# A hash-attention and mixture-of-experts kernel: expert tiles behind a condition, weights by change of expert

## The chip, the cores and the metric

One core of one Trainium2 chip runs the whole program in one launch. The metric is the device time of one execution in microseconds (us); lower is better. The time of the kernel before is the median of three runs. A measurement of this kernel tells about 0.2% from no change.

## The reference

Two blocks follow each other. The first is attention with 4 batches, 8 heads, 768 positions and head width 64, in which a query sees only keys of the same hash bucket. The second sends each of the 3072 tokens (width 512) to the one of 8 experts whose embedding it is most similar to.

```python
q_bits = einsum(q, proj) > 0;  k_bits = einsum(k, proj) > 0      # 6 bits: a bucket
mask = q_bucket[..., :, None] == k_bucket[..., None, :]
attn = softmax(where(mask, q @ k.T / sqrt(D), -1e9))
x = (attn @ v).transpose(0, 2, 1, 3).reshape(3072, 512)
logits = normalized(x) @ normalized(expert_emb).T / tau          # 8 experts
expert_idx = argmax(logits);  gate_w = softmax(logits)[expert_idx]
for e in range(8):
    out[expert_idx == e] = gate_w * (relu(x @ w1[e]) @ w2[e])    # 512 -> 1024 -> 512
```

With the inputs that the reference sets up (a fixed seed), it sends 464, 461, 375, 317, 367, 377, 373 and 338 tokens to the experts 0 to 7.

## The kernel before

**Attention** (lines 166 to 358) takes 16 pairs of heads, each in 12 units of work. A table `todo` in the source says after which unit a pair's loads (`load`), features, hash bits and output (`finish_half`) are issued. SyncE's queue issues the loads of q, k and v; ScalarE makes a pass over a pair's q and k (line 239) and the exps (line 274); TensorE makes the scores (lines 268, 271) and the products with v (line 289). `route` picks an expert for each token and writes the batch's rows, with the gate weight as column 513, to a table `xd` in device memory (line 160).

**The branch.** A general attention, `attention_any`, is needed only when q and k are large. One flag, `beyond_i`, is read into a register by every engine, and a condition (line 446) jumps past that code. With these inputs it isn't run.

**The routing table** (lines 450 to 519) sorts the tokens by expert. TensorE counts (`cnt`, `rank`), VectorE works out for each expert its number of 128-token tiles (`tiles`), their running end (`tend`) and each tile's expert (`texp`), and 24 matmuls (line 516) put the token numbers into slots; `src` (line 519) holds, for each of NT = 31 tiles, 128 row numbers of `xd`. 31 is what 3072 tokens can need at most when each expert's last tile is partly filled. An empty slot points to a row of zeros, and its result is not written.

**The expert tiles** (lines 522 to 576) run 31 times. `fetch(t)` reads the tile's expert into a register of SyncE, loads that expert's `w1t` and `w2t` (2 MB each, lines 535 and 537, two buffers each), and gathers 128 token rows by an indirect DMA of GpSimd (line 539, three buffers). `turn_x` transposes them on TensorE (line 549) and copies them out (VectorE, line 551). 32 products with `w1t` (line 563) go through a Relu on ScalarE in two halves (line 566); 8 products with `w2t` follow (line 571); VectorE scales by the gate weight (`y`, line 573), and GpSimd scatters the rows to the output (line 574). A tile issues `fetch(t + 2)` and `turn_x(t + 1)` between its two products. An fp32 product is two matmul instructions in the trace: 64 of line 563 and 16 of line 571 for a tile.

The pools of weights lie where attention's buffers lay, so no weight load is issued before the routing table is done.

Of the kernel before, what the change touches and what calls it, by code (L numbers as in the profile page):

```python
# [25 lines left out]
def kernel(  # L26
# [26 lines left out]
    NT = (N + E * (P - 1)) // P  # L53
    XW = DM + 1
# [30 lines left out]
    iota_t = iota("iota_t", [P, NT], [[1, NT]])  # L85
# [30 lines left out]
    for h in range(2):  # L116
        for r in range(2):
            c0 = h * D + r * NB
            nc.sync.dma_start(proj2[h * D : (h + 1) * D, c0 : c0 + NB], proj[:, :])

    oh_all = const.tile([P, E, NBLK], F32, name="oh_all")

# [43 lines left out]
    with ExitStack() as at:  # L166
# [3 lines left out]
        op = pool("op", 2, at)  # L170
# [5 lines left out]
        def banks():  # L176
            return ps_w.tile([P, 2, 512], F32, name="banks", tag="banks")
# [4 lines left out]
        for i in range(NPT):  # L182
            t = ep.tile([P, 2, SH + 2], F32, name=f"p{i}")
# [164 lines left out]
        for u in range(U + LAG + 3):  # L348
            if u < U:
                scores(u)  # L350
            if 0 <= u - LAG < U:
                attend(u - LAG)
            for f, *args in todo.get(u, ()):
                f(*args)


        most = rp.tile([P, 1], F32, name="most", tag="most")
        nc.vector.reduce_max(out=most[:], in_=squares[:], axis=AX.X)
        ps = banks()
# [4 lines left out]
                                op0=ALU.is_gt)  # L364
        beyond_i = const.tile([1, 1], I32, name="beyond_i")
# [77 lines left out]
                nc.vector.tensor_copy(out=l[:], in_=lg[:])  # L443
                route(b, x, l, rp)

    with tc.If(nc.values_load(beyond_i[0:1, 0:1], min_val=0, max_val=1) > 0):
        attention_any()


    with ExitStack() as so:  # L450
        sp = pool("sp", 1, so)
# [13 lines left out]
                                in1=iota_n[:].unsqueeze(1).broadcast_to([P, E, NBLK]), op=ALU.is_gt)  # L465
        tiles = sp.tile([P, E], F32, name="tiles")
        nc.vector.reduce_sum(out=tiles[:], in_=full[:], axis=AX.X)
        tend = sp.tile([P, E], F32, name="tend")
        nc.vector.tensor_tensor_scan(out=tend[:], data0=ones[:, 0:E], data1=tiles[:], initial=0.0,
                                     op0=ALU.mult, op1=ALU.add)  # L470
# [3 lines left out]
                                in1=tend[:, 0 : E - 1].unsqueeze(1).broadcast_to([P, NT, E - 1]), op=ALU.is_ge)  # L474
        texp = sp.tile([P, NT], F32, name="texp")
        nc.vector.reduce_sum(out=texp[:], in_=past[:], axis=AX.X)
        texp_i = const.tile([P, NT], I32, name="texp_i")
        nc.vector.tensor_copy(out=texp_i[:], in_=texp[:])


        tstart = sp.tile([P, E], F32, name="tstart")
# [6 lines left out]
                                op=ALU.add)  # L488
# [17 lines left out]
                                in1=rf[:].unsqueeze(2).broadcast_to([P, NBLK, P]), op=ALU.is_equal)  # L506
        col = sp.tile([P, NBLK, NT], F32, name="col")
        nc.vector.tensor_tensor(out=col[:], in0=iota_t[:].unsqueeze(1).broadcast_to([P, NBLK, NT]),
                                in1=tf[:].unsqueeze(2).broadcast_to([P, NBLK, NT]), op=ALU.is_equal)
        nc.vector.tensor_tensor(  # L510
            out=col[:], in0=col[:],
            in1=tok[:].rearrange("p b c -> p (b c)").unsqueeze(2).broadcast_to([P, NBLK, NT]), op=ALU.mult,
# [5 lines left out]
        src = const.tile([P, NT], U32, name="src")  # L518
        nc.vector.tensor_scalar_add(src[:], slot[:], float(N))


    wp = pool("wp", 2)
    gp = pool("gp", 3)
    hp = pool("hp", 2)
    ps_x = pool("ps_x", 2, space=PSUM)
    ps_h = pool("ps_h", 2, space=PSUM)
    ps_y = pool("ps_y", 2, space=PSUM)
    got = {}

    def fetch(t):  # L530
        if t >= NT:
            return
        e = nc.values_load(texp_i[0:1, t : t + 1], engines=(mybir.EngineType.SP,), min_val=0, max_val=E - 1)
        a = wp.tile([P, ND, F], F32, name="w1t", tag="w1t")
        nc.sync.dma_start(a[:], w1[bass.ds(e, 1), :, :].rearrange("o (c p) f -> p (o c) f", p=P))
        b = wp.tile([P, NF, DM], F32, name="w2t", tag="w2t")
        nc.sync.dma_start(b[:], w2[bass.ds(e, 1), :, :].rearrange("o (c p) m -> p (o c) m", p=P))
        x = gp.tile([P, XW], F32, name="xg", tag="xg")
        nc.gpsimd.indirect_dma_start(out=x[:], out_offset=None, in_=xd[:, :],  # L539
                                     in_offset=bass.IndirectOffsetOnAxis(ap=src[:, t : t + 1], axis=0))  # L540
        got[t] = a, b, x

    def turn_x(t):
        if t >= NT:
            return
        a, b, x = got[t]
        ps = ps_x.tile([P, DM], F32, name="ps_x", tag="ps_x")
        for d in range(ND):
            nc.tensor.transpose(ps[:, d * P : (d + 1) * P], x[:, d * P : (d + 1) * P], ident[:])  # L549
        xt = hp.tile([P, ND, P], F32, name="xgt", tag="xgt")  # L550
        nc.vector.tensor_copy(out=xt[:], in_=ps[:].rearrange("p (d n) -> p d n", n=P))  # L551
        got[t] = a, b, x, xt

    fetch(0)
    fetch(1)
    turn_x(0)
    for t in range(NT):
        a, b, x, xt = got.pop(t)
        ht = hp.tile([P, NF, P], F32, name="ht", tag="ht")
        ps = ps_h.tile([P, NF, P], F32, name="ps_h", tag="ps_h")  # L560
        for f in range(NF):
            for d in range(ND):
                nc.tensor.matmul(ps[:, f, :], lhsT=a[:, d, f * P : (f + 1) * P], rhs=xt[:, d, :],  # L563
                                 start=(d == 0), stop=(d == ND - 1))
            if f % 4 == 3:
                nc.scalar.activation(ht[:, f - 3 : f + 1, :], ps[:, f - 3 : f + 1, :], ACT.Relu)  # L566
        fetch(t + 2)
        turn_x(t + 1)
        py = ps_y.tile([P, DM], F32, name="ps_y", tag="ps_y")
        for f in range(NF):  # L570
            nc.tensor.matmul(py[:], lhsT=ht[:, f, :], rhs=b[:, f, :], start=(f == 0), stop=(f == NF - 1))  # L571
        y = gp.tile([P, DM], F32, name="y", tag="y")
        nc.vector.tensor_scalar_mul(y[:], py[:], x[:, DM : DM + 1])  # L573
        nc.gpsimd.indirect_dma_start(out=out[:, :],  # L574
                                     out_offset=bass.IndirectOffsetOnAxis(ap=src[:, t : t + 1], axis=0),
                                     in_=y[:], in_offset=None, bounds_check=N - 1, oob_is_err=False)


# [28 lines left out]
```

## Time and profile before

| | before |
|---|---|
| median of 3 runs | 1033.05 us (1031.98 to 1033.67) |
| the profiled execution, its own time | 1033.62 us |
| its span, first to last instruction | 1031.9 us |
| attention, up to the flag `beyond_i` | 512 us of the span |
| branch and routing table, up to `src` | 512 to 545 us |
| expert tiles, to the last scaling `y` | 545 to 1024 us |
| TensorE busy | 966.8 us (94%) |
| weights loaded for the tiles | 31 times 4 MB |

Times in the profile count from the first instruction. PE is TensorE's matmuls, PEld its weight loads, DVE VectorE, ACT ScalarE, POOL GpSimd, SP SyncE; a q behind a name is that engine's sequencer or DMA queue. PEclk is the granted clock, 1.00 for 2.4 GHz and 0.50 for 1.2 GHz.

### The profile page before, as it was taken

How to read it: one execution, taken by the hardware profiler on the slowest of the kernel's cores; microseconds unless marked ns; L12 is line 12 of the kernel's file. 1: busy time of each engine (PE TensorE's matmuls, PEld its weight loads, DVE VectorE, ACT ScalarE, POOL GpSimd, SP SyncE). 2: the span in 40 equal slices, each digit the busy share in tenths (PEclk: the TensorE clock that was granted, in tenths of full speed). 3: DMA queues.
4: the chain of work that ended last, by engine and by line, in shares of the span. 5: the costliest groups of instructions: out<-in, count | busy, mean ns of one | idle time of the engine just before them, and what ended most of it. 6: DMA issues, size and time to landing. Idle time of an engine off the chain costs nothing. (4 is left out here: it accounts for less than half of the span.)

```text
span 1031.9 us, 13121 instructions
## 1 busy us (share of the span) xinstructions
PE 966.8 (94%) x5477; PEld 574.0 (56%) x5477; DVE 321.0 (31%) x550; ACT 244.9 (24%) x357; POOL 70.0 (7%) x81
## 2 busy tenths in 40 slices
PE   4999999999999999999736999999999999999996
PEld 2444444444444444444335667766766776677674
DVE  3545546554555456455430000100110010011000
ACT  3443444343544335333300000000000000000000
POOL 1000000000000000000001101110110111011000
PEclk8999999999999999999956999999999999999999
DMA  8111013111121112000018988888898888888860
GB/s 184 31 47 46 17 46 107 32 47 47 31 93 47 31 47 77 1 1 1 1 63 313 353 320 310 311 313 316 314 311 317 312 314 312 320 307 314 304 253 1
DMA packets 109121, 170.57 MB, mean 165 GB/s; under 512 B 53302, under 2 KB 57398, under 8 KB 108545
## 3 DMA queue, kind: packets, MB, share of 16 engines
q1 hardware_dynamic: 104064, 155.23, 45.3%
q0 software_dynamic: 4992, 14.44, 3.5%
q8 instruction: 45, 0.74, 0.3%
q14 instruction: 20, 0.16, 0.0%
HBM read 157.06 MB, written 14.43 MB: 166 GB/s over the span
## 5 line engine op out<-in xcount | busy, mean ns | idle before, releaser
L563 PEld LDWEIGHTS ps_h<-xgt,w1t 128*128 128x128 f32 x1984 | 230.5, 193 | 32.4 <-ACT ht L566 18.1
L563 PE MATMUL ps_h<-xgt,w1t 128*128 128x128 f32 x1984 | 236.5, 278 | 10.8 <-ACT ht L566 10.8
L571 PE MATMUL ps_y<-w2t,ht 128*128 128x512 f32 x496 | 218.0, 592 | 0.0
L274 ACT ACTIVATE p<-banks 128x768 f32<-128x768 f32 x192 | 154.0, 808 | 219.6 <-PE banks L271 194.9
L268 PE MATMUL banks<-qt,kt 64*128 64x384 f32 x768 | 177.4, 539 | 0.2 <-ACT p L274 0.2
L289 PE MATMUL av<-p,vt 128*64 128x385 f32 x768 | 166.4, 512 | 0.1
L281 DVE TENSOR_TENSOR acc<-acc,p 128x768 f32<-128x768 f32 x128 | 122.6, 958 | 116.0 <-ACT p L274 114.9
L571 PEld LDWEIGHTS ps_y<-w2t,ht 128*128 128x128 f32 x496 | 91.9, 190 | 103.8 <-issue 103.8
L566 ACT ACTIVATE ht<-ps_h 128x512 f32<-128x512 f32 x62 | 37.0, 597 | 464.2 <-PE ps_h L563 464.2
L573 DVE TENSOR_SCALAR y<-ps_y,xg 128x512 f32<-128x512 f32 x31 | 23.3, 751 | 323.8 <-PE ps_y L571 323.8
L268 PEld LDWEIGHTS banks<-qt,kt 64*128 64x128 f32 x768 | 58.7, 187 | 81.9 <-issue 77.7
L289 PEld LDWEIGHTS av<-p,vt 128*64 128x64 f32 x768 | 38.0, 134 | 91.9 <-issue 89.2
L271 PE MATMUL banks<-qb,kb 64*128 64x384 bf16 x384 | 63.6, 325 | 0.0
L574 POOL DMA_INDIRECT out_dram<-y,src x31 | 31.5, 1015 | 409.4 <-DVE y L573 409.4
L551 DVE COPY xgt<-ps_x 128x512 f32<-128x512 f32 x31 | 21.5, 692 | 110.8 <-PE ps_x L549 100.3
L312 PEld LDWEIGHTS banks<-ones,acc 128*128 128x128 f32 x384 | 51.5, 191 | 0.0
L310 PE MATMUL banks<-iden,o 128*128 128x144 f32 x192 | 47.9, 331 | 0.7 <-DVE o L295 0.7
L312 PE MATMUL banks<-ones,acc 128*128 128x1 f32 x384 | 48.2, 229 | 0.0
L295 DVE TENSOR_SCALAR o<-av 128x384 f32<-128x384 f32 x32 | 19.8, 618 | 68.4 <-PE av L289 68.4
L310 PEld LDWEIGHTS banks<-iden,o 128*128 128x128 f32 x192 | 28.9, 190 | 20.0 <-issue 18.6
L150 POOL TENSOR_TENSOR nrm<-ss,half 128x6 f32<-128x6 f32 x4 | 5.3, 1334 | 488.3 <-ACT sq L132 488.3
L243 PE MATMUL banks<-ident,qk 128*128 128x128 f32 x192 | 29.1, 291 | 8.1 <-DMA qk<-in_q_dram 8.1
(119 smaller groups left out, 417.2 us busy)
## 6 DMA issues: line engine op xcount, KB each, us to landing
w1t<-in_moe_w_dram SPq DMA_DIRECT2D x31, 2048.0 KB, 9.4
w2t<-in_moe_w_dram SPq DMA_DIRECT2D x31, 2048.0 KB, 11.1
xd<-xb SPq DMA_DIRECT2D x4, 1539.0 KB, 5.9
qk<-in_q_dram SPq DMA_DIRECT2D x32, 192.0 KB, 3.6
qk<-in_k_dram SPq DMA_DIRECT2D x32, 192.0 KB, 3.9
vt<-in_v_dram SPq DMA_DIRECT2D x16, 384.0 KB, 3.6
xg<-xd,src POOLq DMA_INDIRECT x31, 7.6
out_dram<-y,src POOLq DMA_INDIRECT x31, 7.7
```

The source lines that it names most:

```text
L243: nc.tensor.transpose(ps[:, c // HC, (c % HC) * P : (c % HC + 1) * P], qk[:, i, c, :, :], ident[:])
L268: nc.tensor.matmul(ps[:, h, 0:SH], lhsT=kt[rows[h], c // HC, kc], rhs=qt[rows[h], s, :], start=True, stop=False)
L271: nc.tensor.matmul(ps[:, h, 0:SH], lhsT=kb[rows[h], c // HC, kc], rhs=qb[rows[h], s, :], start=False, stop=True)
L274: nc.scalar.activation(p[:, :, 0:SH], ps[:, :, 0:SH], ACT.Exp, scale=ESCALE)
L281: nc.vector.tensor_tensor(out=a[:], in0=a[:], in1=p[:, :, 0:SH], op=ALU.add)
L289: nc.tensor.matmul(ps[h * D : (h + 1) * D, 0 : SH + 1], lhsT=vt[:, h, c, :], rhs=p[:, h, 0 : SH + 1], start=(c == 0), stop=(c == NC - 1))
L310: nc.tensor.matmul(t[:, c, :], lhsT=o[:, cols], rhs=iden[:, j, :], start=True, stop=True)
L312: nc.tensor.matmul(z[:, c, h : h + 1], lhsT=a[:, h, cols], rhs=ones[:, 0:1], start=True, stop=True)
L563: nc.tensor.matmul(ps[:, f, :], lhsT=a[:, d, f * P : (f + 1) * P], rhs=xt[:, d, :], start=(d == 0), stop=(d == ND - 1))
L566: nc.scalar.activation(ht[:, f - 3 : f + 1, :], ps[:, f - 3 : f + 1, :], ACT.Relu)
L571: nc.tensor.matmul(py[:], lhsT=ht[:, f, :], rhs=b[:, f, :], start=(f == 0), stop=(f == NF - 1))
L574: nc.gpsimd.indirect_dma_start(out=out[:, :], out_offset=bass.IndirectOffsetOnAxis(ap=src[:, t : t + 1], axis=0), in_=y[:], in_offset=None ...
```

## The change

The weights get four fixed buffers, `w1s` and `w2s`, two each, that live from the start. Expert 0's weights are loaded into all four without a condition, by statements inside the attention loop (after units 48 and 72; a load has no other work to wait for, so the scheduler sets its place in the queue). Six small VectorE steps make three more tables: `live` (tiles that hold tokens), `need` (live tiles whose expert is another than that of the tile two before, whose buffer they take over; for the first two, another than expert 0) and `nt` (the number of live tiles). A weight load is issued for every tile but carried out only if `need` says so (`cond`). It is issued when the buffer's last reader in the tile before is past. Tiles 0 to 23 run as they did; each of tiles 24 to 30 stands inside a condition `nt > t`, nested in that of the tile ahead. The general attention's condition gets `preferred_fallthrough_block=False`: the code of the case that is not run then stands behind the short other case, where before it stood ahead of it. The other pools become fixed turns of as many buffers as before.

```diff
+    NW = 2
+    w1s = [const.tile([P, ND, F], F32, name=f"w1_{i}") for i in range(NW)]
+    w2s = [const.tile([P, NF, DM], F32, name=f"w2_{i}") for i in range(NW)]
+    def bring1(i, e=0, **kw):
+        nc.sync.dma_start(w1s[i][:], w1[bass.ds(e, 1)].rearrange("o (c p) f -> p (o c) f", p=P), **kw)
...
+            if u in (4 * PU, 6 * PU):
+                bring1(u // (2 * PU) - 2)
+                bring2(u // (2 * PU) - 2)
...
-    with tc.If(nc.values_load(beyond_i[0:1, 0:1], min_val=0, max_val=1) > 0):
+    with tc.If(nc.values_load(beyond_i[0:1, 0:1], min_val=0, max_val=1) > 0, preferred_fallthrough_block=False):
         attention_any()
...
+        live = sp.tile([P, NT], F32, name="live")
+        nc.vector.tensor_scalar(out=live[:], in0=iota_t[:], scalar1=tend[:, E - 1 : E], scalar2=None, op0=ALU.is_lt)
+        need = sp.tile([P, NT], F32, name="need")
+        nc.vector.tensor_scalar(out=need[:, 0:NW], in0=texp[:, 0:NW], scalar1=0.0, scalar2=None, op0=ALU.not_equal)
+        nc.vector.tensor_tensor(out=need[:, NW:NT], in0=texp[:, NW:NT], in1=texp[:, 0 : NT - NW], op=ALU.not_equal)
+        nc.vector.tensor_tensor(out=need[:], in0=need[:], in1=live[:], op=ALU.mult)
...
+        nc.vector.tensor_copy(out=nt_i[:], in_=tend[:, E - 1 : E])
...
+    def expert_of(t):
+        e, n = (nc.values_load(a[0:1, t : t + 1], engines=(mybir.EngineType.SP,), min_val=0, max_val=m)
+                for a, m in ((texp_i, E - 1), (need_i, 1)))
+        return e, n > 0
...
+    def expert_tile(t):
...
+        more = t + NW < NT
+        if more:
+            e, needed = expert_of(t + NW)
+            bring1(t % NW, e, cond=needed)
         fetch(t + 2)
         turn_x(t + 1)
...
+        if more:
+            bring2(t % NW, e, cond=needed)
...
+    for t in range(NMIN):
+        expert_tile(t)
+    nt = nc.values_load(nt_i[0:1, 0:1], min_val=NMIN, max_val=NT)
+    with ExitStack() as rest:
+        for t in range(NMIN, NT):
+            rest.enter_context(tc.If(nt > t))
+            expert_tile(t)
```

**SyncE's queue, early attention.** Rows are in program order. `qk_420` and `qk_424` are the loads of pair 3, `qk_601` and `qk_605` those of pair 4. Before:

```order
L226 DMA qk_420<-in_k_dram 128x6x64
L227 DMA vt_421<-in_v_dram 128x2x384
L226 DMA qk_601<-in_q_dram 128x6x64
L226 DMA qk_601<-in_k_dram 128x6x64
L226 DMA qk_601<-in_q_dram 128x6x64
L226 DMA qk_601<-in_k_dram 128x6x64
L227 DMA vt_602<-in_v_dram 128x2x384
```

Now:

```order
L237 DMA qk_424<-in_k_dram 128x6x64
L238 DMA vt_425<-in_v_dram 128x2x384
L127 DMA w1_0_124<-in_moe_w1_dram 128x4x1024
L130 DMA w2_0_126<-in_moe_w2_dram 128x8x512
L127 DMA w1_1_125<-in_moe_w1_dram 128x4x1024
L237 DMA qk_605<-in_q_dram 128x6x64
L237 DMA qk_605<-in_k_dram 128x6x64
L237 DMA qk_605<-in_q_dram 128x6x64
L237 DMA qk_605<-in_k_dram 128x6x64
L130 DMA w2_1_127<-in_moe_w2_dram 128x8x512
L238 DMA vt_606<-in_v_dram 128x2x384
```

Three of the four weight loads now stand ahead of pair 4's q and k, and the fourth right behind them.

**TensorE, from the routing table to tile 1** (`slot` is the table's last product, `ps_x` the transposes, `ps_h` and `ps_y` the two products). Before:

```order
L516 MATMUL slot_3967<-col_3964,row_3962 128x31 x24
L549 MATMUL ps_x_4046<-ident_64,xg_4028 128x128 x4
L549 MATMUL ps_x_4105<-ident_64,xg_4044 128x128 x4
L549 MATMUL ps_x_4178<-ident_64,xg_4103 128x128 x4
L563 MATMUL ps_h_4054<-xgt_4051,w1t_4024 128x128 x32
L571 MATMUL ps_y_4112<-w2t_4026,ht_4053 128x512 x8
```

Now:

```order
L542 MATMUL slot_3985<-col_3982,row_3980 128x31 x24
L574 MATMUL ps_x0_4030<-ident_64,xg0_4020 128x128 x4
L574 MATMUL ps_x1_4031<-ident_64,xg1_4021 128x128 x4
L581 MATMUL ps_h0_4032<-xgt0_4026,w1_0_124 128x128 x16
L574 MATMUL ps_x0_4030<-ident_64,xg2_4022 128x128 x4
L581 MATMUL ps_h0_4032<-xgt0_4026,w1_0_124 128x128 x16
L592 MATMUL ps_y0_4034<-w2_0_126,ht0_4028 128x512 x8
```

The transposes of tile 2 moved from ahead of tile 0's first product to its middle.

**TensorE, the end of tile 23 and the tiles behind it**, now:

```order
L592 MATMUL ps_y1_4035<-w2_1_127,ht1_4029 128x512 x8
L610 TENSOR_LOAD nt_i_3958
L611 COMPARE_AND_BRANCH
L581 MATMUL ps_h0_4032<-xgt0_4026,w1_0_124 128x128 x16
L574 MATMUL ps_x1_4031<-ident_64,xg1_4021 128x128 x4
L581 MATMUL ps_h0_4032<-xgt0_4026,w1_0_124 128x128 x16
L592 MATMUL ps_y0_4034<-w2_0_126,ht0_4028 128x512 x8
L611 COMPARE_AND_BRANCH
```

Before, the same matmuls stood there without a register load or a branch between them.

## Rows read from the trace of the kernel before

**Rows 1.** Profile page: busy time of TensorE over the whole span.

```profile
PE 966.8 (94%) x5477; PEld 574.0 (56%) x5477; DVE 321.0 (31%) x550; ACT 244.9 (24%) x357; POOL 70.0 (7%) x81
```

**Rows 2.** Stretches: length; PE, PEld, DVE, ACT, POOL busy; PEclk, DMA share, GB/s.

```profile
500.00:540.00 40.00, 17.04 (x99) 12.58 (x95) 18.23 (x50) 6.04 (x16) 1.32 (x1) 0.65 0.10 41
...
600.00:700.00 100.00, 97.83 (x570) 71.54 (x569) 10.10 (x14) 7.76 (x13) 13.95 (x14) 1.00 0.89 314
```

**Rows 3.** The same view, 15 us stretches at the end.

```profile
949.00:964.00 15.00, 14.69 (x86) 10.63 (x85) 1.42 (x3) 1.19 (x2) 1.99 (x2) 1.00 0.92 322
964.00:979.00 15.00, 14.69 (x86) 10.63 (x86) 1.42 (x3) 1.19 (x2) 1.99 (x2) 1.00 0.82 298
...
1009.00:1024.00 15.00, 14.00 (x78) 9.63 (x76) 0.73 (x2) 1.19 (x2) 1.00 (x1) 1.00 0.01 1
```

**Rows 4.** Timeline, VectorE: the scaling of tiles 0, 29 and 30 (start, us, instruction).

```profile
573.10 0.75 DVE L573 TENSOR_SCALAR y<-ps_y,xg 128x512 f32<-128x512 f32 x1 [6.18 <-PE ps_y L571]
...
1008.76 0.75 DVE L573 TENSOR_SCALAR y<-ps_y,xg 128x512 f32<-128x512 f32 x1 [10.33 <-PE ps_y L571]
1023.79 0.75 DVE L573 TENSOR_SCALAR y<-ps_y,xg 128x512 f32<-128x512 f32 x1 [14.27 <-PE ps_y L571]
```

**Rows 5.** Timeline, all engines: from the slot table to the first tile's matmuls.

```profile
545.04 0.19 DVE L519 TENSOR_SCALAR src<-slot 128x31 uint32<-128x31 f32 x1 [10.66 <-PE slot L516]
...
545.52 1.06 POOL L539 DMA_INDIRECT xg<-xd,src  x1 [30.20 <-DVE src L519]
...
546.88 0.95 POOL L539 DMA_INDIRECT xg<-xd,src  x1 [0.30 <-issue]
...
552.54 1.09 PE L549 MATMUL ps_x<-ident,xg 128*128 128x128 f32 x4 [7.54 <-DMA xg<-xd,src]
...
556.12 5.49 PE L563 MATMUL ps_h<-xgt,w1t 128*128 128x128 f32 x32
...
562.35 3.84 PE L563 MATMUL ps_h<-xgt,w1t 128*128 128x128 f32 x32 [0.74 <-ACT ht L566]
```

**Rows 6.** The branch at line 446: queue records, ns min/median/max, start.

```profile
L446 PEldq TENSOR_LOAD <-beyond_i x1: 486/486/486, 512.1 to 512.1; - x1
...
L446 PEldq COMPARE_BRANCH  x1: 3507/3507/3507, 512.7 to 512.7; - x1
...
L446 DVEq COMPARE_BRANCH  x1: 72/72/72, 517.4 to 517.4; - x1
L446 DVEq EVENT_SEMAPHORE  x1: 21/21/21, 523.2 to 523.2; - x1
```

**Rows 7.** Timeline, VectorE: first and a small step of the routing table.

```profile
524.49 0.55 DVE L460 TENSOR_TENSOR_SCAN upto<-seg,cnt 128x192 f32<-128x192 f32 x1 [7.55 <-PE cnt L456]
...
527.17 0.18 DVE L478 CAST texp_i<-texp 128x31 int32<-128x31 f32 x1
```

**Rows 8.** Transfers: KB of one, median us from issue to landing.

```profile
w1t<-in_moe_w_dram SPq DMA_DIRECT2D x31, 2048.0 KB, 9.4
...
xd<-zrow POOLq DMA_DIRECT2D x1, 2.0 KB, 2.9
```

**Rows 9.** The chain of waits: the scatter of tile 29.

```profile
1009.79 2.11 DMA out_dram<-y,src
```

**Rows 10.** Stretches, columns as in rows 2: early attention, and first tile.

```profile
25.00:30.00 5.00, 5.00 (x26) 2.05 (x24) 1.70 (x2) 3.93 (x6) 0.00 (x0) 0.77 0.00 0
...
556.00:559.00 3.00, 3.00 (x16) 3.00 (x15) 0.00 (x0) 0.00 (x0) 0.00 (x0) 0.50 1.06 399
```

**Rows 11.** Timeline, SyncE's queue: first load of pair 4.

```profile
35.79 0.54 SPq L226 DMA_DIRECT2D qk<-in_q_dram  x1
```

**Rows 12.** Timeline, ScalarE: the pass over pair 4's q and k, then exps.

```profile
41.67 1.48 ACT L239 ACTIVATE qksq<-qk 128x1536 f32<-128x1536 f32 x1 [2.29 <-DMA qk<-in_k_dram]
...
43.16 1.49 ACT L274 ACTIVATE p<-banks 128x768 f32<-128x768 f32 x2
```

**Rows 13.** Timeline, TensorE: scores that need the first of these exps done.

```profile
45.85 0.92 PE L268 MATMUL banks<-qt,kt 64*128 64x384 f32 x4
```

More of the change, by code (lines that the diff above doesn't have):

```diff
@@ L119, with bring2 @@
             nc.sync.dma_start(proj2[h * D : (h + 1) * D, c0 : c0 + NB], proj[:, :])
+    NW = 2
[3 more added lines that the diff above has]
+        nc.sync.dma_start(w1s[i][:], w1[bass.ds(e, 1)].rearrange("o (c p) f -> p (o c) f", p=P), **kw)
+    def bring2(i, e=0, **kw):
+        nc.sync.dma_start(w2s[i][:], w2[bass.ds(e, 1)].rearrange("o (c p) m -> p (o c) m", p=P), **kw)
     oh_all = const.tile([P, E, NBLK], F32, name="oh_all")
@@ L478 @@
         nc.vector.tensor_copy(out=texp_i[:], in_=texp[:])
+        live = sp.tile([P, NT], F32, name="live")
[4 more added lines that the diff above has]
+        nc.vector.tensor_tensor(out=need[:], in0=need[:], in1=live[:], op=ALU.mult)
+        need_i = const.tile([P, NT], I32, name="need_i")
+        nc.vector.tensor_copy(out=need_i[:], in_=need[:])
+        nt_i = const.tile([P, 1], I32, name="nt_i")
+        nc.vector.tensor_copy(out=nt_i[:], in_=tend[:, E - 1 : E])
         tstart = sp.tile([P, E], F32, name="tstart")
@@ L519, with turns @@
         nc.vector.tensor_scalar_add(src[:], slot[:], float(N))
[L522 to L528, printed above, removed]
-    def fetch(t):
[L531 to L541, printed above, removed]
+    gp = pool("gp", 1)
+    ps = pool("ps", 1, space=PSUM)
+    def turns(p, n, shape, name):
+        ts = [p.tile(shape, F32, name=f"{name}{i}") for i in range(n)]
+        return lambda t: ts[t % n]
+    xg, ys = turns(gp, 3, [P, XW], "xg"), turns(gp, 3, [P, DM], "y")
+    xgt, hts = turns(gp, 2, [P, ND, P], "xgt"), turns(gp, 2, [P, NF, P], "ht")
+    ps_x, ps_h, ps_y = turns(ps, 2, [P, DM], "ps_x"), turns(ps, 2, [P, NF, P], "ps_h"), turns(ps, 2, [P, DM], "ps_y")
+    def expert_of(t):
+        e, n = (nc.values_load(a[0:1, t : t + 1], engines=(mybir.EngineType.SP,), min_val=0, max_val=m)
+                for a, m in ((texp_i, E - 1), (need_i, 1)))
+        return e, n > 0
+    def fetch(t):
+        if t < NT:
+            nc.gpsimd.indirect_dma_start(out=xg(t)[:], out_offset=None, in_=xd[:, :],
+                                         in_offset=bass.IndirectOffsetOnAxis(ap=src[:, t : t + 1], axis=0))
     def turn_x(t):
@@ L545, in turn_x @@
             return
-        a, b, x = got[t]
-        ps = ps_x.tile([P, DM], F32, name="ps_x", tag="ps_x")
         for d in range(ND):
[L549 to L560, printed above, removed]
+            nc.tensor.transpose(ps_x(t)[:, d * P : (d + 1) * P], xg(t)[:, d * P : (d + 1) * P], ident[:])
+        nc.vector.tensor_copy(out=xgt(t)[:], in_=ps_x(t)[:].rearrange("p (d n) -> p d n", n=P))
+    def expert_tile(t):
+        a, b, x, xt, ht, ph, py, y = w1s[t % NW], w2s[t % NW], xg(t), xgt(t), hts(t), ps_h(t), ps_y(t), ys(t)
         for f in range(NF):
             for d in range(ND):
-                nc.tensor.matmul(ps[:, f, :], lhsT=a[:, d, f * P : (f + 1) * P], rhs=xt[:, d, :],
+                nc.tensor.matmul(ph[:, f, :], lhsT=a[:, d, f * P : (f + 1) * P], rhs=xt[:, d, :],
                                  start=(d == 0), stop=(d == ND - 1))
             if f % 4 == 3:
-                nc.scalar.activation(ht[:, f - 3 : f + 1, :], ps[:, f - 3 : f + 1, :], ACT.Relu)
+                nc.scalar.activation(ht[:, f - 3 : f + 1, :], ph[:, f - 3 : f + 1, :], ACT.Relu)
+        more = t + NW < NT
+        if more:
+            e, needed = expert_of(t + NW)
+            bring1(t % NW, e, cond=needed)
         fetch(t + 2)
         turn_x(t + 1)
-        py = ps_y.tile([P, DM], F32, name="ps_y", tag="ps_y")
         for f in range(NF):
             nc.tensor.matmul(py[:], lhsT=ht[:, f, :], rhs=b[:, f, :], start=(f == 0), stop=(f == NF - 1))
-        y = gp.tile([P, DM], F32, name="y", tag="y")
+        if more:
+            bring2(t % NW, e, cond=needed)
         nc.vector.tensor_scalar_mul(y[:], py[:], x[:, DM : DM + 1])
@@ L576 @@
                                      in_=y[:], in_offset=None, bounds_check=N - 1, oob_is_err=False)
+    NMIN = N // P
+    for t in range(NW):
+        e, needed = expert_of(t)
+        bring1(t, e, cond=needed)
+        bring2(t, e, cond=needed)
+        fetch(t)
+    turn_x(0)
+    for t in range(NMIN):
[5 more added lines that the diff above has]
+            expert_tile(t)
 _INS = ['q', 'k', 'v', 'proj', 'moe_expert_emb', 'moe_tau', 'moe_w1', 'moe_w2']
```

## The prediction

> **What bounds the kernel now.** I read the busy times first: TensorE works 94% of the span [rows 1]. An average hides stages, so the stretches came next. Inside the expert tiles TensorE is busy 97.83 of 100 us at full clock, while the DMA engines are at 0.89; between the halves it is busy 17 of 40 us at a mean clock of 0.65 [rows 2]. So the tiles cost what TensorE needs, and what lies between the halves is a chain of waits. Two near-full resources could both set the pace of the tiles, so the third look was at a stretch where one of them is empty. At the end the weight loads stop: from 1009 to 1024 us the core moves 1 GB/s [rows 3], and the last scaling still comes 15.03 us after the one before. From tile 0 to tile 30 the mean is (1023.79 - 573.10) / 30 = 15.02 us [rows 4]. The pace is the same with the transfers gone: TensorE sets it, and fewer weight loads give the steady tiles nothing.
>
> **How many tiles drop out.** The token counts in the reference section, each rounded up to 128, make 4 + 4 + 6 x 3 = 26 tiles. The nearest count to a limit is 377 against 384, so a few tokens decided otherwise change nothing. The trace agrees: from 964 us on, where the scatters of tiles 26 and later are issued, the core moves 298 instead of 322 GB/s [rows 3], 0.36 MB less in 15 us, and a scatter of 128 rows is 0.26 MB. So 5 of 31 tiles compute nothing that is kept, and the condition lets tiles 24 and 25 run.
>
> **The change part by part**, against the profiled execution (1033.62 us, 0.57 above the median):
>
> (a) *Five tiles less.* 5 x 15.02 = **-75.1 us**, all on TensorE's path.
>
> (b) *Weights only when the expert changes.* 14 of the tiles need a pair of loads. Nothing on the path by the argument above: 0. A w1 buffer is read for some 8 us (two runs of 3.84 us and a wait, [rows 5]) of the 30.0 us of two tiles, which leaves 22 us for a load that lands in 9.4 [rows 8]. SyncE's second register read for a tile, 0.49 us at TensorE's price [rows 6], lies in its waits for a buffer.
>
> (c) *First tile.* Before, `src` starts at 545.04, the gather is issued at 545.52 and its data are transposed at 552.54, 7.0 us later; three groups of transposes pass, and the first product starts at 556.12, 11.1 us after `src` [rows 5]. The weights were loading at that time. Now they lie there, and the gather has the DMA engines to itself. Its price is not in the trace: below stand 2.1 us, the scatter of tile 29, which moved nothing beside idle DMA engines [rows 9], above 7.0. Nearest is the 2 KB store of the start, 2.9 us [rows 8]; its 128 x 513 x 4 bytes, 0.26 MB, at the 399 GB/s of the first tile [rows 10] add 0.7, so I take 3.5. The second gather is issued 1.36 us after the first [rows 5] and one group of transposes takes 1.09, so the first product starts 0.48 + 1.36 + 3.5 + 1.09 = 6.4 us after `src`, 4.7 earlier. Tile 2's transposes, now inside tile 0, give 1.1 back: **-3.6 us**, with bounds of -5.0 and -0.1. The Trainium skill, page "DMA: Bandwidth & Descriptors", section "Anatomy of one DMA — SWDGE (gpsimd) path", fits such a transfer as 2.0 us plus its bytes at 436 GB/s; that estimate, 2.6 us, is far below the loaded 7.0 of this trace and would make this term -4.5.
>
> The clock stands at 0.50 when the first tile starts [rows 10]; its first 32 matmuls take 5.49 us against 3.84 [rows 5]. The idle stretch ahead of it remains, so I leave that price in.
>
> (d) *Branch and routing table.* All engines jump at line 446. VectorE compares at 517.4 and shows its next record at 523.2 us; TensorE spends 3507 ns in its compare [rows 6]. `cnt` waits for VectorE, and the table's first step starts at 524.49 [rows 7]. Now the short case follows the compare, so VectorE signals `cnt` at once, but still has to jump past the general attention itself. If that jump costs the same, VectorE arrives at 523.4 and finds `cnt` done: -1.1. If it cost nothing, `cnt` would start with VectorE's signal at 517.5 and the first step 1.1 us behind it, -5.9. Against it stand six more small VectorE steps on the chain, 0.18 us each as the cast of `texp_i` [rows 7]: +1.0, between 0 (in gaps) and 1.6 (at the spacing of dependent steps). I take the jump at its shown price: **-0.1 us**, bounds -5.9 and +1.6.
>
> (e) *Two conditions entered.* TensorE reads `nt` (0.49 us) and compares twice (0.07 as VectorE's compare, [rows 6]): **+0.6 us**. Queued behind are tile 24's matmuls, and everything waits for those. Below: 0.1, if the read runs ahead of the matmuls; above: 3.5 at each, were the code fetched anew, 7.0.
>
> (f) *The end.* From the last scaling to the end of the span pass 1031.9 - 1023.79 = 8.1 us. Now every engine jumps past tiles 26 to 30 there and through the ends of the nested conditions. TensorE's 3.5 us and VectorE's 5.8 lie beside the scatter and its wait; for what GpSimd does one after another I take **+1.0 us**, between 0 and 5.8.
>
> (g) *Weights ahead of pair 4.* The DMA engines idle from 25 us on [rows 10] until pair 4's load at 35.79 [rows 11]. Three weight loads of 2.1 MB at 399 GB/s take 15.8 us; queued behind loads that end by 25, they run from some 24 to 40 us, so the pair's data land some 3 us late. ScalarE, which runs in order, waits for them already (2.29 us, to 41.67) and makes the next two exps only at 43.16 [rows 12]. TensorE needs the first of them done by 45.85 [rows 13]; it ends at 43.16 + 1.49 / 2 = 43.9, so 1.9 of the 3 us are covered: **+0.8 us** with rounding, between 0 and 4.
>
> Sum: -75.1 - 3.6 - 0.1 + 0.6 + 1.0 + 0.8 = -76.4, so 957.2 for the profiled execution and **956.6** for the median. All bounds together reach from 948 to 977; the likeliest case alone, with errors partly cancelling, from 951 to 961.
>
> **Rivals.**
>
> *Fetched code at the conditions.* Each condition entered could stop TensorE as the branch of line 446 did, and the last jump could lie behind the scatter instead of beside it: 956.6 + 6.4 = 963.0 for the first alone, 967.8 with 4.8 more at the end. For it: the 3.5 and 5.8 us in the trace. Against it: those jumps were taken, over long code; a condition entered runs straight on. 0.10. The Trainium skill, page "Runtime: NRT & Kernel Launch", section "Instruction fetch mechanics", says that instructions are prefetched in sequence alone and that a taken branch out of the fetched window stalls the engine; by it the two entered conditions are free and the jump of (d) keeps its price. The trace agrees with the stall, 3507 ns.
>
> *The jump costs nothing* when it is unconditional, (d) at -5.9 + 1.0: 951.8. Nothing in the trace shows such a jump; 0.06.
>
> *Weights ahead disturb attention more* than (g): the fourth load, issued right behind pair 4's, shares the DMA engines with it instead of following it. Its 2.1 MB take 5.3 us, of which nothing is covered any more: 956.6 + 5.3 = 961.9. For it: 16 engines work on all queued transfers. Against it: it is issued last. 0.04.
>
> *Slower than before: conditional loads stall the tiles.* No load of this kind is in the trace. If SyncE works them off slowly, each of 14 loads of w1 stalls TensorE by what exceeds 22 us. From (76.4 + 2) / 14 = 5.6 us of stall each, a landing of 27.6 us, the change is slower than before; at 29 it takes 956.6 + 14 x 7 = 1055. Against it: that is three times the 9.4 us shown, with 14 loads of each kind instead of 31. 0.02.
>
> *The change doesn't do what it says:* `nt` comes out as 31, all tiles run. Then -3.6 - 0.1 + 7 x 0.5 + 1.0 + 0.8 = +1.6, 1034.7. 0.02.
>
> **How the numbers follow.** The forecast has 0.76, the rivals 0.10, 0.06, 0.04, 0.02 and 0.02. The range is 950 to 966: it holds the likeliest case, the free jump, and the half of the fetch rival in which the end stays covered. About 0.2% is what a measurement of this kernel tells from no change. Faster is every case but the last two: 0.96; the last is within 0.2%: 0.02; the slow one 0.02.
>
> **What would show it.** Right: scalings 15.0 us apart throughout, 26 of them; the gather landing in under 4.5 us; the first product about 6.4 us after `src`; no wait over 1 us on TensorE at tiles 24 and 25; some 8 to 10 us from the last scaling to the end. Wrong: TensorE waiting for `w1_0` or `w1_1` in any tile; a gap of 3 us at a condition; a gap near 46 us; scalings closer than 15.0 us, which would mean that the transfers did slow the matmuls.

## The result and the profile after

The changed kernel takes **956.28 us** (median of 4 runs, 956.06 to 957.07), the kernel before 1033.35 us in the same comparison (1031.98 to 1033.67). The ratio is 0.9258, with a 95% interval from 0.9242 to 0.9274. The forecast was 956.6 us. The profiled execution's span went from 1031.9 to 955.3 us, 76.6 us less, where the sum of the prediction was -76.4 (the profiled execution took 957.07 us and is the slowest of the four).

The page of the kernel after: span, busy times, and the queue that carries the weights (packets, MB, share of the DMA engines' time).

```profile
span 955.3 us, 12359 instructions
...
PE 893.7 (94%) x5061; PEld 520.2 (54%) x5061; DVE 314.9 (33%) x547; ACT 239.3 (25%) x347; POOL 62.1 (7%) x73
...
q1 hardware_dynamic: 80544, 92.32, 29.9%
```

TensorE is as busy as before, 94% [rows 1], with 416 fewer matmul instructions. That alone does not say that it sets the pace. Stretches of the kernel after (length; PE, PEld, DVE, ACT, POOL busy; PEclk, DMA share, GB/s) do:

```profile
500.00:540.00 40.00, 16.87 (x99) 11.96 (x95) 18.91 (x57) 6.45 (x16) 1.32 (x1) 0.67 0.10 41
600.00:700.00 100.00, 97.83 (x570) 71.62 (x569) 9.35 (x13) 8.36 (x14) 13.96 (x14) 1.00 0.54 186
```

In the steady tiles TensorE is busy for 97.83 of 100 us, to the hundredth what it was [rows 2], while the transfers fell from 314 to 186 GB/s. A resource that is used by two fifths less without a change of the pace was not setting it. The stretch between the halves is as it was: 17 of 40 us busy, clock 0.67.

VectorE's scalings at the end of tiles 23 to 25, the last three (start, us, instruction):

```profile
914.50 0.75 DVE L595 TENSOR_SCALAR y<-ps_y,xg 128x512 f32<-128x512 f32 x1 [10.33 <-PE ps_y L592]
...
929.52 0.75 DVE L595 TENSOR_SCALAR y<-ps_y,xg 128x512 f32<-128x512 f32 x1 [10.32 <-PE ps_y L592]
...
944.55 0.75 DVE L595 TENSOR_SCALAR y<-ps_y,xg 128x512 f32<-128x512 f32 x1 [10.32 <-PE ps_y L592]
```

They are 15.02 and 15.03 us apart, across the two conditions too. From the first scaling (568.98 us) to the last are 25 periods (a period is the time from one scaling to the next), a mean of 15.023 us, the same as the 30 before [rows 4].

The two profiled executions, cut at the same instructions (us; the starts come from the two timelines):

| stretch | before | after | difference |
|---|---|---|---|
| start to `oh_all` (the last token's expert known) | 515.43 | 516.07 | +0.64 |
| `oh_all` to `upto` (branch, first step of the table) | 9.06 | 8.71 | -0.35 |
| `upto` to `src` (rest of the table) | 20.55 | 21.07 | +0.52 |
| `src` to the first product | 11.08 | 6.96 | -4.12 |
| first product to the first scaling | 16.98 | 16.17 | -0.81 |
| first scaling to the last | 450.69 | 375.57 | -75.12 |
| last scaling to the end | 8.11 | 10.75 | +2.64 |
| sum | 1031.9 | 955.3 | -76.6 |

Three places need their rows. **The first tile**, timeline of all engines:

```profile
545.85 0.19 DVE L545 TENSOR_SCALAR src<-slot 128x31 uint32<-128x31 f32 x1 [10.76 <-PE slot L542]
546.90 1.07 POOL L567 DMA_INDIRECT xg<-xd,src  x1 [30.95 <-DVE src L545]
548.27 0.95 POOL L567 DMA_INDIRECT xg<-xd,src  x1 [0.30 <-issue]
...
550.50 1.09 PE L574 MATMUL ps_x<-ident,xg 128*128 128x128 f32 x4 [4.69 <-DMA xg<-xd,src]
...
551.90 1.11 PE L574 MATMUL ps_x<-ident,xg 128*128 128x128 f32 x4 [0.31 <-DMA xg<-xd,src]
...
552.81 4.69 PE L581 MATMUL ps_h<-xgt,w 128*128 128x128 f32 x32
...
557.34 0.60 PE L574 MATMUL ps_x<-ident,xg 128*128 128x128 f32 x4
...
558.24 3.84 PE L581 MATMUL ps_h<-xgt,w 128*128 128x128 f32 x32 [0.30 <-ACT ht L584]
```

The gather is transposed 3.60 us after its issue (546.90 to 550.50), where it took 7.02 [rows 5]. Tile 2's transposes (557.34) now stand between the halves of tile 0's first product; the pause there is 0.74 us (557.50 to 558.24), the wait for the Relu, and was 0.74 before without them [rows 5]. They cost nothing.

**The branch.** Queue records of line 460 (count, ns min/median/max, first and last start):

```profile
L460 SPq EVENT_SEMAPHORE  x8: 17/17/17, 518.1 to 524.1; - x8
L460 PEldq COMPARE_BRANCH  x2: 95/1716/3337, 513.3 to 513.6; - x2
...
L460 DVEq COMPARE_BRANCH  x2: 51/53/55, 518.0 to 518.2; - x2
...
L460 DVEq EVENT_SEMAPHORE  x1: 21/21/21, 518.1 to 518.1; - x1
```

and the timeline around it:

```profile
518.28 0.98 PE L470 MATMUL cnt<-oh_all,ones 128*128 128x192 f32 x2 [6.77 <-DVEq L460]
...
524.78 0.55 DVE L474 TENSOR_TENSOR_SCAN upto<-seg,cnt 128x192 f32<-128x192 f32 x1 [7.21 <-SPq L460]
```

VectorE now signals at 518.1, before its jump, and `cnt` starts at 518.28 instead of 523.41. Its result lies there for over 5 us: `upto` starts only at 524.78, 0.7 us after the last of SyncE's semaphore events (524.1). The profile puts the wait down to SyncE now, and it is hardly shorter. VectorE's own jump starts at 518.2 (its second compare) and no record shows its end; at the 5.8 us of the kernel before [rows 6] it would end at 524.0, so the two cannot be told apart here.

**The end.** Queue records of the conditions (line 611) and, below, of the program's end (line 640):

```profile
L611 PEldq COMPARE_BRANCH  x4: 65/136/3597, 908.8 to 944.7; - x4
...
L611 POOLq EVENT_SEMAPHORE  x4: 17/43/43, 945.5 to 948.3; - x4
...
L611 POOLq INC_SWDGE_SEM  x1: 1292/1292/1292, 948.4 to 948.4; - x1
```

```profile
L640 POOLq DRAIN  x3: 46/107/4560, 949.9 to 955.0; - x3
```

TensorE's compare that jumps takes 3597 ns, from 938.4 on: its sequencer runs ahead, and the jump lies beside its own last matmuls, which end at 944.5. GpSimd's steps lie one behind another: the scatter of the output rows (issued at 945.58), the semaphore wait (to 948.3), an increment of 1.29 us, the jump, and a drain of 4.56 us from 949.9 on.

### The profile page after: what moved, and what is told of

It reads as the page before. It is cut to its first block, busy times and chain, and to the rows that moved or that the text cites. A ratio compares the mean times of both kernels' runs of the same rounds, so it can differ in the third digit from the quotient of the medians.

```text
span 955.3 us, 12359 instructions
## 1 busy us (share of the span) xinstructions
PE 893.7 (94%) x5061; PEld 520.2 (54%) x5061; DVE 314.9 (33%) x547; ACT 239.3 (25%) x347; POOL 62.1 (7%) x73
## 5 line engine op out<-in xcount | busy, mean ns | idle before, releaser
L581 PEld LDWEIGHTS ps_h<-xgt,w 128*128 128x128 f32 x1664 | 192.8, 193 | 26.5 <-ACT ht L584 14.6
L581 PE MATMUL ps_h<-xgt,w 128*128 128x128 f32 x1664 | 197.8, 277 | 8.4 <-ACT ht L584 8.4
L592 PE MATMUL ps_y<-w,ht 128*128 128x512 f32 x416 | 182.8, 592 | 0.0
L584 ACT ACTIVATE ht<-ps_h 128x512 f32<-128x512 f32 x52 | 31.0, 597 | 390.4 <-PE ps_h L581 390.4
L592 PEld LDWEIGHTS ps_y<-w,ht 128*128 128x128 f32 x416 | 77.1, 190 | 87.0 <-issue 87.0
L595 DVE TENSOR_SCALAR y<-ps_y,xg 128x512 f32<-128x512 f32 x26 | 19.5, 750 | 268.2 <-PE ps_y L592 268.2
L575 DVE COPY xgt<-ps_x 128x512 f32<-128x512 f32 x27 | 18.7, 692 | 92.9 <-PE ps_x L574 84.5
L596 POOL DMA_INDIRECT out_dram<-y,src x26 | 26.5, 1020 | 337.6 <-DVE y L595 324.9
```

The lines of the kernel that those rows point to most:

```text
L581: nc.tensor.matmul(ph[:, f, :], lhsT=a[:, d, f * P : (f + 1) * P], rhs=xt[:, d, :], start=(d == 0), stop=(d == ND - 1))
L584: nc.scalar.activation(ht[:, f - 3 : f + 1, :], ph[:, f - 3 : f + 1, :], ACT.Relu)
L596: nc.gpsimd.indirect_dma_start(out=out[:, :], out_offset=bass.IndirectOffsetOnAxis(ap=src[:, t : t + 1], axis=0), in_=y[:], in_offset=None ...
```

## The experiments

Every kernel was timed in three rounds against the kernel before, which took 1033.6 to 1033.8 us (medians) in these batches. The stages in the texts are those of the table above; each is an edit of the kernel after, or of the run ahead where the text says so.

### Which part of the change pays

**Loads always.** The weights of every tile are loaded, as before, but into the fixed buffers.

```diff
-            bring1(t % NW, e, cond=needed)
+            bring1(t % NW, e)
...
-            bring2(t % NW, e, cond=needed)
+            bring2(t % NW, e)
```

> The change, but every tile from tile 2 on loads its weights again, as before; the five dead tiles stay skipped. If TensorE alone sets the pace of a tile, the scalings stay 15.02 us apart and the time stays at 956.3 us within 0.7. If the transfers that no longer run gave something, the tiles lengthen: with 0.1 us for each of 25 periods it is 958.8 us, with 0.3 us 964.

961.75 us (ratio 0.9304, 0.9288 to 0.9319), so 5.5 us slower than the kernel after. The period is 15.023 us still: the transfers in the tiles are worth nothing. But the last scaling to the end takes 15.82 us instead of 10.75. SyncE's queue, then stretches behind the last scaling (944.08), then TensorE's compares and GpSimd's increment at the conditions:

```profile
937.20 0.37 SPq L127 DMA_DIRECT2D w<-in_moe_w_dram  x1
944.07 0.37 SPq L130 DMA_DIRECT2D w<-in_moe_w_dram  x1
```

```profile
945.00:950.00 5.00, 0.00 (x0) 0.00 (x0) 0.00 (x0) 0.00 (x0) 1.02 (x1) 0.67 0.92 298
950.00:955.00 5.00, 0.00 (x0) 0.00 (x0) 0.00 (x0) 0.00 (x0) 0.00 (x0) 0.50 0.48 184
```

```profile
L611 PEldq COMPARE_BRANCH  x4: 65/136/6777, 908.3 to 944.9; - x4
...
L611 POOLq INC_SWDGE_SEM  x1: 1292/1292/1292, 953.1 to 953.1; - x1
```

The loads issued inside tiles 24 and 25 are for tiles 26 and 27, which do not run. They still move 298 and 184 GB/s when all arithmetic is over, and GpSimd's increment comes at 953.1 instead of 948.4. TensorE's compare with the jump, from 937.9 on, takes 6777 ns beside the first of them, and 3597 without; it ends at 944.7, and the scatter is issued 1.03 us behind the last scaling, as in the kernel after, so it adds nothing. I had not thought of loads that outlive the work.

**Loads for live tiles only.** This tells the two halves of the mask apart: the load is done for every tile that runs, also when its expert is already in the buffer.

```diff
-        nc.vector.tensor_tensor(out=need[:, NW:NT], in0=texp[:, NW:NT], in1=texp[:, 0 : NT - NW], op=ALU.not_equal)
+        nc.vector.memset(need[:, NW:NT], 1.0)
```

> Every live tile from tile 2 on loads its weights, also when the expert stays; dead tiles load nothing. The run that loaded for every tile lost 5.1 us, all behind the last scaling, where the loads of tiles 26 and 27 were still under way. If those two dead loads are the whole loss, this run ends 10.7 us after its last scaling, at 956.3 us within 0.8. If repeated loads as such cost time, it stays near 961 us.

956.84 us (0.9257, 0.9241 to 0.9272), last scaling to end 10.74. The mean period is 15.040 us, with two periods of 25 that are 0.2 us longer; such periods come in runs that skip loads too (mean 15.043 in the run with the last store behind the branch and the old layout), and why is open. All of the 5 us of the run ahead were the two dead tiles' loads. Loading "only when the expert changes" is worth nothing clear of noise here; the factor `live` in the mask is what counts.

**All 31 tiles,** with everything else of the change.

```diff
-            rest.enter_context(tc.If(nt > t))
```

> The change without the seven conditions: all 31 tiles run. If the five tiles are the gain, 5 x 15.02 = 75.1 us come back, less the 2.6 us by which the change's end is longer than that of the kernel before if the nested conditions are its cause: 1028.8 us, or 1031.4 us if they are not. If the weight loads that are skipped or ahead were a larger share than 5 us, it stays under 1025 us.

1030.54 us (0.9965, 0.9953 to 0.9978). The five tiles are 74.3 us of the 77 gained. Without the conditions the end takes 8.05 us, as before, instead of 10.75, so the nested conditions are what made it longer. The time is nearer to the 1031.4 us that was expected if they were not. In the profiled execution three periods are 0.25 to 0.3 us longer (mean 15.050, 0.8 us in all), and the first tile takes 1.0 us more from first product to first scaling, because the clock rose later; together they take back 1.8 us.

### Weights ahead and the first tile

**Weights not ahead:** the first four loads are issued once the table knows the experts.

```diff
-            if u in (4 * PU, 6 * PU):
-                bring1(u // (2 * PU) - 2)
-                bring2(u // (2 * PU) - 2)
...
-        bring1(t, e, cond=needed)
-        bring2(t, e, cond=needed)
+        bring1(t, e)
+        bring2(t, e)
```

> The weights keep buffers of their own, but nothing is loaded during attention: tiles 0 and 1 load theirs as soon as the tile table is there, at about 529 us. Four loads at 399 GB/s take 21 us and end at about 550 us. If the gain at the first tile comes from a gather that has the DMA engines to itself, the gather (issued at 546.9 us) still meets the last load, and the first product starts 0 to 3 us later: 956.3 to 959.3 us. If having the weights early in attention is what counts, the first product waits, 960 us or more. Attention itself should be no faster: its 0.65 us belongs to the clock.

**Weights in attention's room:** the edit of the run ahead, and the four buffers come from a pool that lies where attention's buffers lay, as before the change.

```diff
+    wp = pool("wp", 1)
+    w1s += [wp.tile([P, ND, F], F32, name=f"w1_{i}") for i in range(NW)]
+    w2s += [wp.tile([P, NF, DM], F32, name=f"w2_{i}") for i in range(NW)]
     gp = pool("gp", 1)
```

> As the run before, but the weights' buffers lie again where attention's buffers lay, so that their first loads wait for the end of the routing table, as in the kernel before. If weight traffic beside the gather is what the first tile lost, the first product starts 11.1 us after the row numbers instead of 7.0, and tile 0 takes 17.0 us: 956.3 + 4.9 = 961.2 us. If the order of the transposes or the clock made that gain, it stays under 958 us.

Not ahead: 959.2 us (0.9283, 0.9267 to 0.9298), 2.9 slower than the kernel after. In attention's room: 961.52 us (0.9308, 0.9292 to 0.9323), 5.2 slower. The timelines show when the last weight load was issued, and how long the first gather took. Not ahead:

```profile
531.95 2.44 SPq L130 DMA_DIRECT2D w<-in_moe_w_dram  x1
...
545.72 1.07 POOL L564 DMA_INDIRECT xg<-xd,src  x1 [30.84 <-DMA w<-in_moe_w_dram]
...
552.23 1.94 PE L571 MATMUL ps_x<-ident,xg 128*128 128x128 f32 x8 [7.60 <-DMA xg<-xd,src]
```

In attention's room:

```profile
544.78 1.07 POOL L566 DMA_INDIRECT xg<-xd,src  x1 [30.38 <-DVE src L541]
...
550.90 2.41 SPq L129 DMA_DIRECT2D w<-in_moe_w_dram  x1
...
552.56 2.17 PE L573 MATMUL ps_x<-ident,xg 128*128 128x128 f32 x8 [8.29 <-DMA xg<-xd,src]
```

The gather takes 6.51 and 7.78 us, against 3.60 with no weights under way; the first product comes 9.44 and 11.79 us after `src`, against 6.96. The second is the 11.08 of the kernel before, brought back by loading late into buffers in attention's room. This is term (c), shown from both sides.

### The branch in the middle

**The old layout of the branch.**

```diff
-    with tc.If(..., preferred_fallthrough_block=False):
+    with tc.If(...):
```

> The change, but with the general attention's condition laid out as before. If VectorE's first step of the routing table waits for the store of the last batch's rows, which lands at 524.1 us, the layout matters by no more than the count that comes 1 us behind the jump: 956.3 to 956.8 us. If the jump is what it waits for, 957.4 us.

957.07 us (0.9259, 0.9244 to 0.9275). Its runs, 956.58 to 957.66 us, overlap with those of the kernel after, and the median lies between the two that were expected, so the time decides nothing. `upto` comes 9.04 instead of 8.71 us behind `oh_all`. VectorE's records:

```profile
L460 DVEq COMPARE_BRANCH  x1: 72/72/72, 516.4 to 516.4; - x1
L460 DVEq EVENT_SEMAPHORE  x1: 21/21/21, 522.3 to 522.3; - x1
```

5.9 us pass over the jump, as in the kernel before (5.8, [rows 6]). With this layout `cnt` waits for the jump, with the other `upto` waits beside it.

**No general attention at all.**

```diff
-    with tc.If(nc.values_load(beyond_i[0:1, 0:1], min_val=0, max_val=1) > 0, preferred_fallthrough_block=False):
-        attention_any()
```

> Leaves out the general attention and its condition altogether; with these inputs it isn't run. If the store of the last batch gates the routing table, because the table's buffers lie where the stored rows lay, the first step stays where it is, and the time falls by no more than 0.7 us: 955.6 to 956.3 us. If the branch and its jumps are the price, VectorE starts the table right after its last attention step, 6 us earlier: 950 us.

948.62 us (0.9181, 0.9165 to 0.9196), 7.7 less than the kernel after. The branch is 6.58 us of that by the trace; the profiled execution also reaches `oh_all` 2.5 us sooner, which is within what attention varies by between these kernels. Timeline:

```profile
513.58 0.27 DVE L155 TENSOR_TENSOR oh_all<-iota_e,idx 128x48 f32<-128x48 f32 x1
...
514.00 0.98 PE L468 MATMUL cnt<-oh_all,ones 128*128 128x192 f32 x2 [3.38 <-DVE oh_all L155]
...
515.71 0.55 DVE L472 TENSOR_TENSOR_SCAN upto<-seg,cnt 128x192 f32<-128x192 f32 x1 [0.21 <-PE rank L470]
...
517.75 0.34 SPq L171 DMA_DIRECT2D xd<-xb  x1
```

`upto` starts 2.13 us after `oh_all`, 6.58 sooner than with the branch, and 2.04 us before the last store of `xd` is even issued (517.75). So nothing of the table itself waits for that store: what holds it up is how the branch is left.

**The last store behind the branch.** The last batch's rows lie in a buffer of their own, and SyncE stores them to `xd` after the branch (`big` is the flag, read by all engines as before) instead of in `route`.

```diff
+    last_x = const.tile([P, NC, XW], F32, name="last_x")
...
-    with tc.If(nc.values_load(beyond_i[0:1, 0:1], min_val=0, max_val=1) > 0, preferred_fallthrough_block=False):
+    big = nc.values_load(beyond_i[0:1, 0:1], min_val=0, max_val=1)
+    with tc.If(big > 0, preferred_fallthrough_block=False):
         attention_any()
+    small_i = nc.values_load(beyond_i[0:1, 0:1], engines=(mybir.EngineType.SP,), min_val=0, max_val=1)
+    store(B - 1, last_x, cond=small_i < 1)
```

> The last batch's rows get a buffer of their own, and their store is issued behind the general attention's condition (carried out if that was not run). If the store gates the routing table, VectorE's first step comes as soon as its jump is done: 0.9 us earlier if the jump takes 5.7 us whatever else moves (955.4 us), up to 6 us earlier if the jump was slow only beside the store (950.5 us). If the store has nothing to do with it, 956.3 us.

**The same with the old layout,** against the run ahead.

```diff
-    with tc.If(big > 0, preferred_fallthrough_block=False):
+    with tc.If(big > 0):
```

> The last batch's store behind the general attention's condition, as in the run before that tried it, with the condition laid out as in the kernel before. If that layout counts once the store is out of the way, the routing table's first step comes 1 us later than with the new layout, 6.1 us behind the expert table instead of 5.1, and the time is 954.5 us. If the layout never counts, 953.5 us.

953.55 us (0.9221, 0.9205 to 0.9236) and 953.82 us (0.9228, 0.9212 to 0.9243). Both beat the kernel after and the kernel before: their runs (at most 954.81 us) lie below all runs of the kernel after (from 956.06). `upto` comes 5.15 and 5.09 us after `oh_all`, so 3.56 us of the branch's 6.58 go when the store is no longer under way, and 3.95 with the old layout (from 9.04). The layout no longer counts. The 953.55 us lie between the two times that were expected with the store as the cause, since the jump gets shorter but keeps a price. In both runs VectorE's last four steps of attention, 1.36 us from `l` to `upto`, also moved behind the jump; they are part of the 5.1 us. Timeline of the first, then VectorE's records of the second:

```profile
519.65 0.21 DVE L164 TENSOR_TENSOR l<-l,nrm 128x48 f32<-128x48 f32 x1 [3.48 <-issue]
...
520.84 0.39 SPq L175 DMA_DIRECT2D xd<-last_x  x1
521.01 0.55 DVE L482 TENSOR_TENSOR_SCAN upto<-seg,cnt 128x192 f32<-128x192 f32 x1 [0.20 <-issue]
```

```profile
L466 DVEq COMPARE_BRANCH  x1: 72/72/72, 516.2 to 516.2; - x1
L466 DVEq EVENT_SEMAPHORE  x1: 21/21/21, 519.1 to 519.1; - x1
```

What is left is VectorE's jump: it compares at 516.2 and goes on at 519.1, 2.9 us, where it took 5.8 and 5.9 us beside the store. The store held up two things, which end within a microsecond of each other: SyncE's wait at the branch's end, and VectorE's longer jump. Both go with the store; these runs do not tell which of the two alone would have kept `upto` back.

### The end

**Tiles 24 and 25 without a condition,** and no tiles behind them, which with these inputs is the same work (NMIN is 24).

```diff
-    nt = nc.values_load(nt_i[0:1, 0:1], min_val=NMIN, max_val=NT)
-    with ExitStack() as rest:
-        for t in range(NMIN, NT):
-            rest.enter_context(tc.If(nt > t))
-            expert_tile(t)
+    for t in range(NMIN, NMIN + 2):
+        expert_tile(t)
```

> Leaves out the run-time choice of tiles: 26 tiles without a condition, for these inputs alone. The change needs 10.7 us from the last scaling to the end, the kernel before 8.1. If leaving the nested conditions costs the difference, 8.1 us return and the time is 953.7 us. If it is the last scatter, which now moves rows where it moved none before, the end stays at 10.7 us and the time at 956.3 us.

953.19 us (0.9221, 0.9205 to 0.9236), 3.1 less. From the last scaling to the end it takes 7.42 us instead of 10.75; the period is 15.022, so the conditions cost nothing where tiles run and 3.3 us where they end. VectorE's last scaling, and GpSimd's drain:

```profile
943.68 0.75 DVE L595 TENSOR_SCALAR y<-ps_y,xg 128x512 f32<-128x512 f32 x1 [10.33 <-PE ps_y L592]
```

```profile
L637 POOLq DRAIN  x3: 40/112/5828, 944.5 to 950.9; - x3
```

The drain is no shorter (5828 against 4560 ns) but starts at 944.5, 0.8 us after the scaling, and so lies beside the landing of the scatter. In the kernel after, GpSimd first waits for that landing, makes its increment (there is none in the run without conditions) and jumps: its drain starts 5.35 us after the scaling. The last scatter moves rows here as in the kernel after, so moved rows do not explain the longer end.

## Why the prediction was right

(a) *Five tiles less*, -75.1: measured -75.12 by the trace, and 74.3 us by putting the tiles back, where the end is 2.7 us shorter.

(b) *Weights by change of expert*, 0: shown by the run that loads always, with an unchanged period of 15.023 us. The reasoning went from one stretch without traffic [rows 3]; that was enough. It missed that a load of a tile that does not run would have cost 5 us at the end. The change avoids that, so the sum was not touched.

(c) *First tile*, -3.6: the gather landed in 3.60 us, where 3.5 was taken between 2.1 and 7.0. The Trainium skill, page "DMA: Bandwidth & Descriptors", section "Anatomy of one DMA — SWDGE (gpsimd) path", gives 2.0 us plus the bytes at 436 GB/s, by estimate 2.6 us; the trace disagrees by 1.0 us, and the sum of the smallest store and the bytes at the rate of this trace was nearer. The first product came 6.96 us after `src`, not 6.4: the gather was issued 1.05 us after `src` instead of 0.48. The loads ahead are not the cause, since it is 1.05 too where nothing is loaded ahead; it is 0.48 again with the weights in attention's room and without the general attention, and why is open. Two things came out better. The 1.1 us of tile 2's transposes were not given back, since they lie in the wait for the Relu. And the stretch from first product to first scaling lost 0.81 us. That part is luck. Stretches from the first product on, of the kernel after and, below, of the run with the old layout of the branch, whose first tile is the same:

```profile
552.81:554.81 2.00, 2.00 (x11) 2.00 (x11) 0.69 (x1) 0.00 (x0) 0.00 (x0) 0.50 0.03 10
554.81:557.50 2.69, 2.69 (x26) 2.69 (x26) 0.00 (x0) 0.00 (x0) 0.00 (x0) 1.00 0.00 0
```

```profile
551.49:554.99 3.50, 3.50 (x18) 3.50 (x18) 0.69 (x1) 0.00 (x0) 0.00 (x0) 0.50 0.02 5
```

The first tile starts at the low clock, 0.50, as the prediction assumed and as before [rows 10]. In the kernel after the clock stood at 1.00 from 2.0 us behind the first product on, and the first 32 matmuls took 4.69 us instead of the 5.49 before; with the old layout it was still 0.50 for 3.5 us, and they took 5.49. Together -4.9 instead of -3.6, of which -4.1 come from the earlier first product.

(d) *Branch and table*, -0.1: measured -0.35 + 0.52 = +0.17. The six small steps cost half of the 1.0 taken. With the old layout the jump kept its price (5.9 us); in the kernel after no record shows its end. The -1.1 from the earlier `cnt` came to a third. 0.7 us pass between 524.1, where SyncE's last event stands and where a jump at the old price would about end, and `upto`; the prediction had not read SyncE's wait, and what fills the 0.7 is open. The Trainium skill, page "Runtime: NRT & Kernel Launch", section "Instruction fetch mechanics", has a taken branch out of the fetched window stall its engine; the traces agree with a stall, with 2.9 to 5.9 us on VectorE and 3.3 to 3.9 on TensorE at this branch, and TensorE's compares that do not jump at 0.07 to 0.10 us. That the time goes into fetching, no run here shows.

(e) *Two conditions entered*, +0.6: measured 0. Scalings stayed 15.02 us apart. TensorE's queue reads the register for `nt` at 908.4 us, while tile 23's matmuls are still running, so the read is covered; that was the lower bound, 0.1. The rival of fetched code at each condition falls with it.

(f) *The end*, +1.0: measured +2.64, inside its bounds of 0 and 5.8; the end, 10.75 us, lies outside the 8 to 10 that the prediction named as its sign. The step that was mis-sized is what GpSimd does "one after another": it held the semaphore wait and increment, but I had not seen that its drain, until then beside the scatter's landing, would move behind them.

(g) *Weights ahead of pair 4*, +0.8: the delay came, its price did not (and the prediction's own numbers, 1.9 of 3 us covered, leave 1.1). Timeline of ScalarE in the kernel after, then the same pass with the old layout of the branch:

```profile
42.79 0.81 ACT L285 ACTIVATE p<-banks 128x768 f32<-128x768 f32 x1 [2.48 <-DVE qb L268]
44.59 0.81 ACT L285 ACTIVATE p<-banks 128x768 f32<-128x768 f32 x1 [0.99 <-DVE acc L292]
45.30 1.48 ACT L250 ACTIVATE qksq<-qk 128x1536 f32<-128x1536 f32 x1
```

```profile
44.30 1.49 ACT L250 ACTIVATE qksq<-qk 128x1536 f32<-128x1536 f32 x1 [0.46 <-DMA qk<-in_k_dram]
```

With the old layout pair 4's data are there at 44.30, where they were there at 41.67 before the change [rows 12], so they did come late by about what was forecast. But the pass over them now stands behind two exps in ScalarE's order, and in the kernel after it waits for nothing (45.30). The prediction had kept the old order. The stretch up to `oh_all` did get 0.64 us longer, but that is no cost of the loads: over the kernels run, `oh_all` came at 513.6 to 516.1 us, at 514.5 (old layout of the branch) with the weights ahead and at 514.5 and 515.0 (the two runs of the section on weights) without. In the stretch from 25 to 30 us the clock was 0.58, where it was 0.77 [rows 10]:

```profile
25.00:30.00 5.00, 5.00 (x22) 1.98 (x22) 1.59 (x2) 3.79 (x5) 0.00 (x0) 0.58 1.02 399
```

TensorE's scores that stood at 33.05 us stand at 33.96, ahead of anything of pair 4, and behind pair 4's pass, at 46.77 instead of 45.85, they are no later than that. Why the clock rose later is open.

So the two terms that carry the total, (a) and (c), were right for the reasons given. That the sum is right to 0.3 us is luck in part: the terms other than (a) were each off by up to 1.6 us, with both signs, and cancel: (c) -1.3, (d) +0.3, (e) -0.6, (f) +1.6, (g) -0.2. In them are two amounts that the change does not set, 0.81 us less in (c) and 0.64 more counted under (g), both of which vary as much between the kernels run.

## What to carry to other kernels

Work that is skipped by a condition saves what it costs on the bound resource, here 15.02 us a tile, and the conditions themselves cost little where they are entered; look for their price where they end, on the engine that waits for transfers, and where they are left by a jump. A transfer that is hidden is not worth skipping, except where nothing follows it: there the dead load is the last work of the kernel. Before a branch that all engines take, let no large store be under way; and what a first transfer costs after an idle stretch is to be read off a quiet place of the trace, not off its busy twin.

## What the runs showed that I had not expected

- The same jump of VectorE past the same code takes 5.8 to 5.9 us while the store of 1.6 MB (768 x 513 x 4 bytes) is under way and 2.9 us without it; TensorE's jump at the end takes 3.3 to 3.8 us over the kernels run, and 6.8 beside a dead load of 2 MB.
- Leaving a condition in which GpSimd has issued a scatter makes GpSimd wait for the landing and then spend 1.29 us on an increment; with the drain behind it, not beside it, 3.3 us at the end of this kernel.
- A 0.26 MB gather takes 3.6 to 3.8 us, from issue to its first transpose, without weight loads and 6.5 to 7.8 us beside 8 MB of weight loads.
- The first 32 matmuls of the first tile, the same instructions, take 4.4 to 5.8 us over the kernels run, by when the granted clock rises; this alone spreads the time from first product to first scaling from 15.87 to 17.30 us, more than several of the terms that were forecast.
